# Cosine attention and a leaky-ReLU MLP: weight quarters and four pairs of heads moved in the order of loads

## The chip, the cores and the metric

The kernel runs on one core of one Trainium2 chip. Its metric is the device time of one execution, in microseconds (us), lower is better. Six actors matter: TensorE (PE in the profile, its weight loads PEld), VectorE (DVE), ScalarE (ACT), GpSimd (POOL), SyncE (SP), which only issues transfers, and the 16 DMA engines that carry them out.

## The reference

What is computed, for q, k and v of 8 batches x 12 heads x 448 rows x 64 and an MLP with 768 x 2048 and 2048 x 768 weights:

```python
q_n = q / (np.linalg.norm(q, axis=-1, keepdims=True) + 1e-06)
k_n = k / (np.linalg.norm(k, axis=-1, keepdims=True) + 1e-06)
scores = np.matmul(q_n, k_n.transpose(0, 1, 3, 2)) / tau
attn = np.exp(scores - scores.max(-1, keepdims=True))
attn = attn / (attn.sum(-1, keepdims=True) + 1e-09)
x = np.matmul(attn, v)           # then (batch*row, head*dim) = 3584 x 768
h = x @ w_in
out = np.maximum(0.01 * h, h) @ w_out
```

## The kernel before

**Slots.** A slot is one pair of heads of one batch: 8 batches x 6 pairs are 48 slots, counted from 0, so "the 13th to 16th pair" are slots 12 to 15. Per slot the kernel

- loads q and k: `load_qk(s)` (L119) issues four transfers on SP's queue, the first 384 rows of q, those of k, and the 64 rows that remain of each;
- squares them on POOL: `squares(s)` (L156), which must wait until the slot's loads have landed;
- sums the squares on DVE: `sums(s)` (L169), in two parts, q and k;
- takes the roots on ACT: `roots(s)` (L180), and normalises to bf16 on DVE: `normalise(s)` (L190);
- transposes the result: `transposes(s)` (L226), on TensorE up to slot 9 and by a DMA transpose on SP's queue from slot 10 on;
- multiplies for the scores, three key tiles of 128 rows per slot and one that two slots share, and takes their exponentials on ACT: `key_tiles` (L245).

`hold(x)` (L485) is a one-column copy on POOL that reads a normalised slot. POOL executes in order, so what is written behind it starts no earlier than that slot was normalised.

**Groups.** Two slots make a group of four heads. `load_v(j)` (L138) and `load_v_rem` (L145) load a group's values, cast to bf16 on the way, on POOL's queue. `totals(j)`, `products(j, e)` and `scale(j, e)` make the sums of the exponentials, the products with v and the quotient, which is the MLP's input, transposed.

**Weights.** `load_w_in(i)` (L104) loads a quarter of w_in (768 KB as bf16): quarters 0 and 1 hold the even and the odd row blocks of the first half of its columns, 2 and 3 those of the second half. `load_w_out(half)` (L110) loads half the columns of w_out (1536 KB). Both run on POOL's queue.

**Order of the work.** The order on every engine is written out by hand.

1. A loop over slots s = 0 to 5 (L528 to L588) does the first batch's attention. Iteration s normalises slot s + 1, issues the loads of slot s + 5, squares slot s + 3, and sums slot s + 2; the q part of that sum stands on DVE ahead of the normalisation (L541 to L543). v's groups 1 and 2, w_in's quarters 1 to 3 and both halves of w_out are issued in it too, behind that iteration's squares on POOL (L550 to L557). Group 0 of v and quarter 0 of w_in are issued just ahead of the loop (L513, L514).
2. `firsts(b, begun, between)` (L634) multiplies one "chunk" of x (384 or 512 of the rows of two batches, in turn) by w_in: 16 blocks m of its columns, each with 6 products and one activation on ACT. `between` says what else is put ahead of which m. For batch 0 slots 6 to 9 are normalised in it.
3. `visit(b, order, norms, between)` (L644) multiplies a chunk by w_out in groups of two output blocks of 128 rows and half the columns (`two_groups`, L413). A group goes over the 16 row blocks of w_out twice, and the scores of the next batch's six slots are put between its steps; the scores of slots 12 and 13, and of 14 and 15, against their shared keys come first in visit 1 (L649). After the 4th step of the first `norms` groups, `norm` (L623) normalises one slot, issues the loads of the slot four further on and squares the slot two further on; after the 20th step the next slot is summed (L658 to L661).
4. `attend_batch(b + 1)`, the v loads of the batch after, and `firsts(b + 1, ...)` follow, with further slots normalised (L700 to L715). Then 3 and 4 again.

In visit 0 the first group of two uses w_out's first half only, the second group both halves (L693).

**Buffers.** q and k have four buffers, so slot s + 4 can be loaded once slot s has been normalised; the normalised slots have three, the transposed ones five.

Of the kernel before, what the change touches and what calls it, by code (L numbers as in the profile page):

```python
# [16 lines left out]
def kernel(  # L17
# [23 lines left out]
    MT = D_ff // 128  # L41
    HALF = D_model // 2
# [24 lines left out]
    gp = nc.gpsimd  # L67
# [32 lines left out]
    w_out_sb = cpool.tile([128, MT, D_model], BF16, name="w_out_sb")  # L100
    w_in_r = moe_w_in.rearrange("(j p e) n -> e p j n", p=128, e=2)
    w_out_r = moe_w_out.rearrange("(mo mi) n -> mi mo n", mi=128)

    def load_w_in(i):  # L104
        n0, e = i // 2 * (D_ff // 2), i % 2
        gp.dma_start(
            out=w_in_sb[:, e::2, n0 : n0 + D_ff // 2], in_=w_in_r[e, :, :, n0 : n0 + D_ff // 2]
        )

    def load_w_out(half):  # L110
        n0 = half * HALF
        gp.dma_start(out=w_out_sb[:, :, n0 : n0 + HALF], in_=w_out_r[:, :, n0 : n0 + HALF])

    def main(x, b, h0, nh):
        return x[b, h0 : h0 + nh, 0:MAIN].rearrange("h (p t) d -> p h t d", t=3)
# [3 lines left out]
    def load_qk(s, engs=(nc.sync, nc.sync), rem_eng=None):  # L119
        if s >= NSLOT:  # L120
            return
        b, h0 = s // NPAIR, 2 * (s % NPAIR)
        q_h = ldp.tile([128, 2, 4, D], F32, name="q_h")
        k_h = ldp.tile([128, 2, 3, D], F32, name="k_h")
        engs[0].dma_start(out=q_h[:, :, 0:3], in_=main(q, b, h0, 2))
        engs[1].dma_start(out=k_h, in_=main(k, b, h0, 2))
        for i, (x, eng) in enumerate(zip((q, k), engs)):
            (rem_eng or eng).dma_start(  # L128
                out=q_h[64 * i : 64 * i + 64, :, 3],
                in_=x[b, h0 : h0 + 2, MAIN:S].rearrange("h p d -> p h d"),  # L130
            )
        raw[s] = (q_h, k_h)
# [5 lines left out]
    def load_v(j):  # L138
        if j >= B * NQ:
            return  # L140
        b, jj = divmod(j, NQ)
        vb[j] = vbp.tile([128, 4, 3, D], BF16, name="v_b")
        gp.dma_start(out=vb[j], in_=main(v, b, 4 * jj, 4))  # L143
# [12 lines left out]
    def squares(s, engs=(gp, gp)):  # L156
        if s >= NSLOT:
            return
        tiles = []
        for x, eng, name in zip(raw[s], engs, ("sq0", "sq1")):  # L160
            sq = sqp.tile(list(x.shape), F32, name=name)
            if eng is nc.scalar:
                nc.scalar.activation(sq, x, func=AF.Square)
            else:
                eng.tensor_tensor(sq, x, x, op=ALU.mult)  # L165
            tiles.append(sq)
        sqs[s] = tiles

    def sums(s, parts=(0, 1)):  # L169
        if s >= NSLOT:  # L170
            return
        if s not in ss:
            ss[s] = smp.tile([128, 14], F32, name="ss")
        for i in parts:
            o = ss[s][:, 0:8] if i == 0 else ss[s][:, 8:14]
            nc.vector.tensor_reduce(  # L176
                o.rearrange("p (h t) -> p h t", h=2), sqs[s][i], axis=AX.X, op=ALU.add
            )

    def roots(s):  # L180
        if s >= NSLOT:
            return
        nc.scalar.activation(ss[s], ss[s], func=AF.Ln, bias=tiny)  # L183
        nc.scalar.activation(ss[s], ss[s], func=AF.Exp, scale=0.5)  # L184
        if s < 2:
            nc.scalar.activation(ss[s], ss[s], func=AF.Identity, bias=eps)  # L186
# [55 lines left out]
    def scores(s, kis):  # L242
        key_tiles([(s, ki) for ki in kis])
# [231 lines left out]
    def fill(count):  # L475
        wm = banks(1)
        for i in range(count):
            nc.tensor.matmul(
                out=wm, lhsT=warm[:, :128], rhs=warm, start=(i == 0), stop=(i == count - 1)
            )  # L480
# [4 lines left out]
    def hold(x):  # L485
        seen = smp.tile([128, 1], F32, name="seen")
        gp.tensor_copy(out=seen, in_=x)  # L487
# [21 lines left out]
    normalise(0)  # L509
    load_qk(4)  # L510
    hold(qn[0][:, 6, 0, 0:1])
    squares(2)
    load_v(0)  # L513
    load_w_in(0)  # L514
    dst = qtp.tile([128, 7, 128], BF16, name="qkT")
    qkT[0] = dst.rearrange("p t c -> p (t c)")
# [11 lines left out]
    for s in range(NPAIR):  # L528
        j = s // 2 - 1 if s >= 2 else None
        even = s % 2 == 0  # L530
        n = s + 2 if s + 2 < NPAIR else None
        if s != 3 and s != 5:
            scores(s, (0,))
        if s == 1:
            roots(2)
        if j is not None and not even:
            products(j, 1)
        scores(s, (1,))
        fill(2)
        if s and n:  # L540
            sums(n, (0,))  # L541
        if s < 5:
            normalise(s + 1)  # L543
            load_qk(s + 5)
        if j is not None and not even:
            scale(j, 0)
        if s < 5:
            hold(qn[s + 1][:, 6, 0, 0:1])
            squares(s + 3)
        if s in (1, 2):  # L550
            load_v(s)
        if s == 0:
            load_v_rem(0, slice(2, 4))
        if s < 3:
            load_w_in(s + 1)
        if s in (3, 4):
            load_w_out(s - 3)  # L557
        if n:
            sums(n, (1,))
        scores(s, (2,))  # L560
        if s == 5:

            scale(j, 1)
            for m in range(SOON):
                pms[0, m] = banks(1, (0, m, 0), 4 + m)
            first(0, 0, range(KT - 2))
        elif not even:
            fill(2)
        if not even:
            scores(s, (3,))  # L570
        if s < 5:
            transposes(s + 1)
        if s == 0:
            sums(2, (0,))
        if s == 5:
            first(0, 1, range(KT - 2))
            sums(6)
            sums(7)
        elif not even:
            fill(2)  # L580
        if n and s:
            roots(n)
        if j is not None and not even and s < 5:
            scale(j, 1)
        if j is not None and even:
            totals(j)
            scores(s + 1, (0,))
            products(j, 0)  # L588
# [34 lines left out]
    def norm(s, transposed=True):  # L623
        if s >= NSLOT:
            return
        roots(s)
        normalise(s)
        if transposed:
            transposes(s)
        load_qk(s + 4)  # L630
        hold(qn[s][:, 6, 0, 0:1])
        squares(s + 2)

# [10 lines left out]
    def visit(b, order, norms, between):  # L644


        s0 = (b + 1) * NPAIR
        tiles = [(s0 + p, ki) for p in range(NPAIR) for ki in range(3)]
        key_tiles([(s0 + 1, 3), (s0 + 3, 3)])  # L649
        for i, two in enumerate(order):  # L650
            after = between[i == len(order) - 1]
            for n, _ in enumerate(two_groups(b, two), 1):
                for _ in range(after.get(n, 0)):
                    key_tiles([tiles.pop(0)])
                if not tiles and s0 + 5 not in ended:
                    ended.add(s0 + 5)
                    key_tiles([(s0 + 5, 3)])
                if n == 4 and i < norms:  # L658
                    norm(s0 + 4 + i)
                if n == 20 and i < norms:  # L660
                    sums(s0 + 5 + i)  # L661
        assert not tiles

# [19 lines left out]
    ready = 10  # L683
    for b in range(B):
        tokens = chunk_cols(b)[1] // 128
        if b == B - 1:
            for ts in range(tokens):
                for half in range(2):
                    second(b, ts, half)
            break  # L690
        order = [((ts, 0), (ts, 1)) for ts in range(tokens)]
        if b == 0:
            order = [((0, 0), (1, 0)), ((2, 0), (0, 1)), ((1, 1), (2, 1))]  # L693
        visit(b, order, tokens - 1, three if tokens == 3 else four)
        ready += tokens - 1
        attend_batch(b + 1)
        for j in range((b + 2) * NQ, (b + 3) * NQ):
            load_v(j)
        load_v_rem(b + 2)
        s = ready  # L700
        between = {0: [lambda s=s: norm(s)], 1: [lambda s=s: sums(s + 1)]}
        if tokens == 3:
            between.update({
                4: [lambda s=s: norm(s + 1), lambda s=s: sums(s + 2)],
                7: [lambda s=s: norm(s + 2), lambda s=s: sums(s + 3)],
                10: [lambda s=s: norm(s + 3)], 13: [lambda s=s: sums(s + 4)],
            })
            ready += 4
        else:
            between.update({  # L710
                4: [lambda s=s: norm(s + 1)], 5: [lambda s=s: sums(s + 2)],
                8: [lambda s=s: norm(s + 2)], 12: [lambda s=s: sums(s + 3)],
            })
            ready += 3
        firsts(b + 1, 0, between)  # L715
# [35 lines left out]
```

## Time and profile before

| | us |
|---|---|
| median of 3 runs | 419.67 |
| the three runs | 417.07, 419.67, 420.43 |
| the profiled execution | 417.26 |
| its span, first to last instruction | 415.4 |
| TensorE busy in it | 401.8 (97%) |
| ScalarE busy | 260.1 (63%) |
| VectorE busy | 193.4 (47%) |
| GpSimd busy | 138.1 (33%) |

The trace is of the profiled execution; its instants are counted from the first instruction. TensorE's granted clock is 0.996 of full speed on the mean. A row of the timeline gives start, length, engine, line, operation, what it writes from what it reads, and in brackets how long the engine stood idle before it and what ended that. A row with "SPq", or one on POOL with DMA_DIRECT2D, is the issue of a transfer; the rows "... KB, n" give the time from that issue to the landing. In the chain of waits a DMA's length counts from its issue to its landing.

### The profile page before, as it was taken

What the parts mean: (1) busy time and instruction counts of PE and PEld (TensorE: products, weight loads), DVE (VectorE), ACT (ScalarE), POOL (GpSimd) and SP (SyncE); (2) the same over time, 40 slices, a digit from 0 to 9 for tenths busy, and PEclk for the clock granted to TensorE, in tenths of its full rate; (3) what the DMA queues carried; (4) which work ended last, traced back from release to release, by engine and by line L of the source; (5) the groups of instructions that cost most, each with busy time, mean ns of one, the idle gap of its engine ahead of it and who ended that gap; (6) DMA issues with size and microseconds to landing.
All of it is one profiled execution on the core that took longest, in us unless ns stands there. A gap on an engine that the chain in (4) does not pass through costs nothing.

```text
span 415.4 us, 10159 instructions
## 1 busy us (share of the span) xinstructions
PE 401.8 (97%) x4088; PEld 215.0 (52%) x4099; DVE 193.4 (47%) x412; ACT 260.1 (63%) x448; POOL 138.1 (33%) x209
## 2 busy tenths in 40 slices
PE   8689997999999999999999999999999999999996
PEld 3224655544555555544555555544555565544564
DVE  6865965256352735157261645156362654040021
ACT  4877477745785569845775559855776559934300
POOL 2935457055140634054231533153232530000000
PEclk9999999999999999999999999999999999999999
DMA  6999999886376965576376975576477753210023
GB/s 149 201 220 220 221 221 197 206 114 148 86 191 131 113 156 128 124 116 141 91 177 144 115 172 95 136 110 136 109 171 163 102 97 50 75 39 2 0 76 77
DMA packets 104911, 54.21 MB, mean 130 GB/s; under 512 B 70816, under 2 KB 99872, under 8 KB 104864
## 3 DMA queue, kind: packets, MB, share of 16 engines
q1 hardware_dynamic: 78960, 41.24, 42.8%
q0 software_dynamic: 25056, 11.80, 22.5%
q8 instruction: 32, 0.52, 0.5%
q10 hardware_dynamic: 848, 0.52, 0.4%
q14 instruction: 15, 0.12, 0.1%
HBM read 45.61 MB, written 11.01 MB: 136 GB/s over the span
## 4 chain that ended last, share of the span: by engine, by line
PE 83%; DMA 13%; SPq 1%; DVE 1%; ACT 1%; POOL 0%; issue 0%; POOLq 0%; ACTq 0%
PE ps L355 31%; PE ps L434 29%; PE ps L297 10%; PE ps L257 7%; DMA w_out_sb<-in_moe_w_out_dram 7%; PE ps L392 5%; DMA q_h<-in_k_dram 4%; DMA k_h<-in_k_dram 2%; PE ps L284 1%; SPq L128 1%; POOL sq L165 0%; DVE qn L200 0%; DVE ss L176 0%; ACT ss L183 0%; ACT ss L186 0%
## 5 line engine op out<-in xcount | busy, mean ns | idle before, releaser
L355 PE MATMUL ps<-xT,w_in_sb 128*128 128x384 bf16 (+1 forms) x760 | 147.3, 352 | 0.4
L434 PE MATMUL ps<-w_out_sb,hT 64*128 64x384 bf16 x1536 | 143.5, 323 | 2.1 <-DMA w_out_sb<-in_moe_w_out_dram 2.1
L269 ACT ACTIVATE pe<-ps 128x896 bf16<-128x896 f32 x144 | 123.3, 918 | 22.5 <-PE ps L257 20.8
L362 ACT ACTIVATE hT<-ps 128x384 bf16<-128x384 f32 (+1 forms) x128 | 67.7, 544 | 73.5 <-PE ps L355 73.2
L355 PEld LDWEIGHTS <-w_in_sb 128*128 128x128 bf16 x768 | 74.2, 98 | 71.2 <-issue 3.4
L434 PEld LDWEIGHTS <-hT 64*128 64x128 bf16 x1536 | 75.1, 94 | 56.3 <-issue 5.8
L444 DVE COPY osb<-ps 128x384 f32<-128x384 f32 x48 | 24.5, 553 | 76.9 <-PE ps L434 43.7
L257 PE MATMUL ps<-qkT 64*128 64x448 bf16 (+1 forms) x384 | 55.5, 354 | 3.4 <-ACT pe L269 2.0
L176 DVE TENSOR_REDUCE ss<-sq 128x6 f32<-128x384 f32 (+1 forms) x95 | 54.7, 611 | 4.7 <-POOL sq L165 4.4
L165 POOL TENSOR_TENSOR sq<-q_h 128x512 f32<-128x512 f32 x46 | 48.5, 1055 | 18.1 <-DMA q_h<-in_k_dram 17.4
L487 POOL CAST seen<-qn 128x1 f32<-128x1 bf16 x48 | 8.9, 185 | 124.2 <-DVE qn L200 120.4
L143 POOL DMA_DIRECT2D v_b<-in_v_dram x24 | 18.6, 775 | 66.9 <-PE ps L297 66.9
L195 DVE TENSOR_SCALAR ss<-ss 128x14 f32<-128x14 f32 x46 | 8.2, 178 | 68.5 <-ACT ss L184 68.5
L165 POOL TENSOR_TENSOR sq<-k_h 128x384 f32<-128x384 f32 x46 | 39.0, 848 | 0.0
L332 DVE TENSOR_TENSOR xT<-ps,rb 128x448 bf16<-128x448 f32 x48 | 27.8, 620 | 23.1 <-ACT rb L311 23.0
L200 DVE TENSOR_TENSOR qn<-q_h,r 128x512 bf16<-128x512 f32 x48 | 34.7, 723 | 1.6
L297 PE MATMUL ps<-pe,v_b 128*32 128x448 bf16 x576 | 31.9, 353 | 0.0
L257 PEld LDWEIGHTS <-qkT 64*128 64x128 bf16 (+1 forms) x384 | 17.7, 96 | 23.8 <-issue 11.1
L200 DVE TENSOR_TENSOR qn<-k_h,r 128x384 bf16<-128x384 f32 x48 | 28.8, 600 | 0.0
L310 ACT ACTIVATE rb<-ps 128x448 f32<-128x448 f32 x24 | 12.9, 539 | 24.3 <-PE ps L297 24.3
L398 DVE COPY osb<-ps 128x384 f32<-128x384 f32 (+1 forms) x9 | 4.6, 513 | 36.6 <-issue 22.6
L269 ACT ACTIVATE pr<-ps 128x896 bf16<-128x896 f32 x24 | 21.3, 921 | 0.2 <-PE ps L257 0.2
(49 smaller groups left out, 216.8 us busy)
## 6 DMA issues: line engine op xcount, KB each, us to landing
q_h<-in_q_dram SPq DMA_DIRECT2D x48, 192.0 KB, 3.2
k_h<-in_k_dram SPq DMA_DIRECT2D x46, 192.0 KB, 3.1
out_dram<-osb SPq DMA_DIRECT2D x30, 192.0 KB, 3.0
v_b<-in_v_dram POOLq DMA_DIRECT2D x24, 192.0 KB, 4.7
out_dram<-osb SPq DMA_DIRECT2D x12, 384.0 KB, 2.8
w_in_sb<-in_moe_w_in_dram POOLq DMA_DIRECT2D x4, 768.0 KB, 12.9
w_out_sb<-in_moe_w_out_dram POOLq DMA_DIRECT2D x2, 1536.0 KB, 24.1
q_h<-in_q_dram SPq DMA_DIRECT2D x48, 32.0 KB, 3.8
```

The source lines that it names most:

```text
L165: eng.tensor_tensor(sq, x, x, op=ALU.mult)
L176: nc.vector.tensor_reduce(o.rearrange("p (h t) -> p h t", h=2), sqs[s][i], axis=AX.X, op=ALU.add)
L200: nc.vector.tensor_tensor(qn[s][:, lo:hi], x.rearrange("p h t d -> p t h d"), r[:, r0 : r0 + 2 * nt].rearrange("p (h t) -> p t h", h=2) .u ...
L257: nc.tensor.matmul(out=out[:, a, :S], lhsT=x[rows, c0:c1], rhs=x[rows, 0:S], start=True, stop=True,)
L269: nc.scalar.activation(out=dst, in_=sc[:, :, :S], func=AF.Exp, scale=inv_tau)
L297: nc.tensor.matmul(out=x[32 * g : 32 * g + 32, :S], lhsT=weights(g, ki) if ki < 3 else rem(g), rhs=pe[s][:, ki, a, :] if ki < 3 else pr[j] ...
L332: nc.vector.tensor_tensor(xT[m][:, 2 * jj + e, half * S : (half + 1) * S], pos.pop((j, e))[:, :S], rbs[j], op=ALU.mult,)
L355: nc.tensor.matmul(out=pm[:, :n], lhsT=w_in_sb[:, kt, m * 128 : (m + 1) * 128], rhs=xT[c // 2][:, kt, c0 : c0 + n], start=(kt == 0), stop= ...
L362: nc.scalar.activation(out=hT[c][:, m, :n], in_=pms.pop((c, m))[:, :n], func=AF.Prelu, alpha=0.01)
L392: nc.tensor.matmul(out=po2[:, :n], lhsT=hT[c][:, m, ts * 128 : (ts + 1) * 128], rhs=w_out_sb[:, m, lo : lo + n], start=(m == 0), stop=(m = ...
L434: last[i] = nc.tensor.matmul(out=po2[:, i, :HALF], lhsT=hT[c][rows, m, ts * 128 : (ts + 1) * 128], rhs=w_out_sb[rows, m, half * HALF : (ha ...
L444: nc.vector.tensor_copy(out=osb[c, ts][:, half * HALF : (half + 1) * HALF], in_=po2[:, i, :HALF])
```

## The change

- `load_w_out` can split its half into several transfers, each with a run of the 16 row blocks; the second half is issued in four.
- Group 0 of v is issued ahead of `squares(2)` instead of behind it.
- Quarters 1, 2 and 3 of w_in are issued in iterations 1, 2 and 3 instead of 0, 1 and 2. Group 2 of v is issued in iteration 3 instead of 2. The halves of w_out stay in iterations 3 and 4.
- `norm(8)` and `norm(9)`, in the first `firsts`, no longer issue the loads of slots 12 and 13; `norm(10)` and `norm(11)`, in visit 0, do, where those of slots 14 and 15 were. Slots 14 and 15 load ahead of m = 0 of the second `firsts`.
- The sum of slot 12 leaves visit 0 for m = 1 of that `firsts`, and slots 12 to 15 are normalised ahead of m = 2, 5, 8 and 11, where it was 0, 4, 7 and 10. From slot 16 on all is issued by the same rule as before.

```diff
-    def load_w_out(half):
-        n0 = half * HALF
-        gp.dma_start(out=w_out_sb[:, :, n0 : n0 + HALF], in_=w_out_r[:, :, n0 : n0 + HALF])
+    def load_w_out(half, parts=1):
+        n0, n = half * HALF, MT // parts
+        for m in range(0, MT, n):
+            gp.dma_start(
+                out=w_out_sb[:, m : m + n, n0 : n0 + HALF],
+                in_=w_out_r[:, m : m + n, n0 : n0 + HALF],
+            )
...
     hold(qn[0][:, 6, 0, 0:1])
+    load_v(0)
     squares(2)
-    load_v(0)
     load_w_in(0)
...
-        if s in (1, 2):
-            load_v(s)
+        if s in (1, 3):
+            load_v(s // 2 + 1)
         if s == 0:
             load_v_rem(0, slice(2, 4))
-        if s < 3:
-            load_w_in(s + 1)
-        if s in (3, 4):
-            load_w_out(s - 3)
+        elif s < 4:
+            load_w_in(s)
+        if s == 3:
+            load_w_out(0)
+        elif s == 4:
+            load_w_out(1, 4)
...
-        load_qk(s + 4)
+        if not 8 <= s < 12:
+            load_qk(s + 4)
+        elif s >= 10:
+            load_qk(s + 2)
         hold(qn[s][:, 6, 0, 0:1])
         squares(s + 2)
...
-                if n == 20 and i < norms:
+                if n == 20 and i < norms - (b == 0):
                     sums(s0 + 5 + i)
...
-        if tokens == 3:
+        if b == 0:
+            between = {
+                0: [lambda: load_qk(14), lambda: load_qk(15)],
+                1: [lambda: sums(12)], 2: [lambda: norm(12)],
+                3: [lambda: sums(13)], 5: [lambda: norm(13)],
+                6: [lambda: sums(14)], 8: [lambda: norm(14)],
+                9: [lambda: sums(15)], 11: [lambda: norm(15)], 13: [lambda: sums(16)],
+            }
+            ready += 4
+        elif tokens == 3:
```

## The prediction

> **What bounds the kernel now.** I read the chain that ended last, then the busy time of each engine stage by stage, then the instants at which TensorE waits.
>
> ```profile
> PE 83%; DMA 13%; SPq 1%; DVE 1%; ACT 1%; POOL 0%; issue 0%; POOLq 0%; ACTq 0%
> ```
> ```profile
> 26.38:29.80 3.42, 1.98 (x14) 0.78 (x15) 3.36 (x8) 1.37 (x4) 1.35 (x3) 1.00 1.26 219
> 29.80:33.21 3.41, 3.41 (x27) 1.27 (x25) 1.96 (x4) 2.29 (x3) 2.43 (x3) 0.50 1.12 225
> 33.21:63.80 30.59, 30.41 (x304) 17.05 (x302) 21.30 (x41) 21.34 (x42) 16.26 (x22) 1.00 1.24 221
> 63.80:65.93 2.13, 0.00 (x1) 0.00 (x1) 2.06 (x5) 0.72 (x3) 2.13 (x5) 1.00 1.37 233
> 65.93:106.50 40.57, 40.47 (x397) 21.32 (x402) 19.06 (x38) 24.76 (x42) 16.38 (x24) 1.00 0.88 162
> 106.50:411.90 305.40, 304.99 (x3211) 166.71 (x3216) 128.44 (x277) 190.72 (x323) 83.99 (x127) 1.00 0.54 111
> ```
> ```profile
> 38.46 27.42 DMA w_out_sb<-in_moe_w_out_dram
> 65.93 0.97 PE ps L434 x9
> ```
>
> The columns of a stage are its length, then the busy time of PE, PEld, DVE, ACT and POOL, the granted clock, the DMA share and GB/s. From 65.93 us to the end TensorE is busy 40.47 of 40.57 and 304.99 of 305.40 us: a change can win nothing there, only lose. All that can be won lies before 65.93 us: 2.13 us in which TensorE does nothing until w_out's second half, 27.42 us on its way, has landed; and a head in which it is busy 1.98 of 3.42 us and then works 3.41 us at half clock. DMA moves 219 to 233 GB/s through all of this: the head is a queue for the DMA engines.
>
> **How the two queues share them.** Packets of POOL's queue (q0) and of SP's (q1), from 22 to 26 us beside w_in, and from 40 to 64 us beside w_out:
>
> ```profile
> q0 software_dynamic: 342, 0.66, 87.3%
> q1 hardware_dynamic: 351, 0.20, 22.9%
> ```
> ```profile
> q0 software_dynamic: 4010, 3.07, 81.3%
> q1 hardware_dynamic: 4021, 2.19, 43.0%
> ```
>
> They go one for one. A pair of packets takes 4000/342 = 11.7 ns beside w_in and 24000/4010 = 6.0 ns beside w_out. A slot (one pair of heads) is 2 x 192 KB in rows of 768 B and 2 x 32 KB in rows of 256 B, 768 packets. So a q/k load is slow when w_in lies beside it, which is what the order of issues decides.
>
> **Part 1: w_out's second half.** Slots 12 and 13 no longer load in front of it: 1536 packets. SP's part of a pair is 43.0/(81.3 + 43.0) = 35% of 6.0 ns, 2.1 ns, so 3.2 us of traffic leave, and the half would land near 62.7 us even whole. In quarters, the first four of its sixteen row blocks land some three quarters of its 12.4 us of service (its landing at 65.9 less that of the first half, below) earlier. TensorE asks at 63.80. The wait of 2.1 us goes: **-2.1**, with both causes covering it. If the head below wins time, TensorE asks earlier; the quarters cover that.
>
> w_out's first half must be there at 57.12, where its products begin:
>
> ```profile
> 32.81 1.21 POOL L112 DMA_DIRECT2D w_out_sb<-in_moe_w_out_dram  x1
> ...
> 38.46 1.20 POOL L112 DMA_DIRECT2D w_out_sb<-in_moe_w_out_dram  x1
> 43.28 0.18 POOL L487 CAST seen<-qn 128x1 f32<-128x1 bf16 x1 [3.62 <-DVE ss L195]
> ```
> ```profile
> w_out_sb<-in_moe_w_out_dram POOLq DMA_DIRECT2D x1, 1536.0 KB, 20.7
> ```
>
> ```profile
> 57.12 0.99 PE L434 MATMUL ps<-w_out_sb,hT 64*128 64x384 bf16 x10
> ```
>
> It lands at 32.81 + 20.7 = 53.5, 3.6 us early. The bytes ahead of it in its queue stay the same, so I leave it there. Three more issues on POOL cost between nothing and 3 x 1.20 = 3.6 us; behind them stand slot 6's hold and slot 8's squares, and POOL idles 3.62 us just there: 0.
>
> The price of a transfer, whatever its size, could speak against quarters. Four small loads issued back to back at 84.48 us:
>
> ```profile
> 84.48 2.45 POOL L150 DMA_DIRECT2D v_rem<-in_v_dram  x4
> ```
> ```profile
> v_rem<-in_v_dram POOLq DMA_DIRECT2D x2, 32.0 KB, 3.4
> ```
>
> All four are issued within 2.45 us and each lands some 3.4 us after its own issue, so they overlap; I take 0 for the split, and 3 x 3.4 = 10.2 us as the far end. The Trainium skill ("DMA: Bandwidth & Descriptors", Anatomy of one DMA) puts a fixed 2.0 us on every DMA; three more in a row would make 6.0 us by it, the last quarter near 68.7. The trace's overlapping landings do not bear out adding them up.
>
> **Part 2: the head.** Slot 0's v load (L513) now issues before squares(2), so w_in(0), at 12.35 us today, issues some 0.7 us sooner: v's issue (0.8 us) is out from between. Then it stands ahead of slot 4's last transfer, and w_in(1), which ran beside slot 5's, stands an iteration later. What these two loads do today:
>
> ```profile
> 12.15 0.60 SPq L128 DMA_DIRECT2D q_h<-in_k_dram  x1
> ...
> 14.61 0.66 SPq L128 DMA_DIRECT2D q_h<-in_k_dram  x1
> ```
> ```profile
> q_h<-in_k_dram SPq DMA_DIRECT2D x1, 32.0 KB, 3.7
> ```
> ```profile
> q_h<-in_k_dram SPq DMA_DIRECT2D x1, 32.0 KB, 9.5
> ```
> ```profile
> 12.35 0.76 POOL L106 DMA_DIRECT2D w_in_sb<-in_moe_w_in_dram  x1
> ...
> 17.51 1.03 POOL L165 TENSOR_TENSOR sq<-q_h 128x512 f32<-128x512 f32 x1
> ...
> 24.24 1.03 POOL L165 TENSOR_TENSOR sq<-q_h 128x512 f32<-128x512 f32 x1 [3.09 <-DMA q_h<-in_k_dram]
> ```
> ```profile
> 20.42 0.81 PE L214 MATMUL ps<-id,qn 128*128 128x128 bf16 x7 [0.39 <-DVE qn L200]
> ...
> 27.16 0.81 PE L214 MATMUL ps<-id,qn 128*128 128x128 bf16 x7 [1.15 <-DVE qn L200]
> ```
> ```profile
> 18.58 0.69 DVE L176 TENSOR_REDUCE ss<-sq 128x8 f32<-128x512 f32 x1 [0.34 <-POOL sq L165]
> ...
> 25.31 0.69 DVE L176 TENSOR_REDUCE ss<-sq 128x8 f32<-128x512 f32 x1 [3.41 <-POOL sq L165]
> ```
> ```profile
> 26.06 0.92 ACT L269 ACTIVATE pr<-ps 128x896 bf16<-128x896 f32 x1
> 28.60 0.31 ACT L183 ACTIVATE ss<-ss,tiny 128x14 f32<-128x14 f32 x1 [1.62 <-DVE ss L176]
> ```
>
> Slot 4 lands at 12.15 + 3.7 = 15.9, slot 5 at 14.61 + 9.5 = 24.1. DVE sums slot n+1 before it normalises slot n, so a late load stops the slot before it: 3.41 us at 25.31 for slot 5. ACT, which runs without a pause up to 26.98, then waits 1.62 us.
>
> After the change slot 4 lands between 15.9 (as now) and 12.15 + 9.5 = 21.7 (treated as slot 5 is). I take 18.5: q/k issue ahead of w_in(0) and go first, the remainders (256 packets) go beside it at 11.7 ns, 3.0 us. Its squares then start at 18.65 instead of 17.51, and everything up to ACT's 26.98 moves by 1.1, to 28.1: the new stall is at slot 3's transposition, 0.39 + 1.1 us. Slot 5 follows slot 4 with no w_in beside it; with the 3.7 us that slot 4 takes so, it lands near 22.2, not 24.1, and slot 4's transposition is ready 27.16 - 24.24 = 2.9 us after its squares start, at 25.3, before TensorE comes to it. The wait of 1.62 us goes, and ACT goes on at 28.1 instead of 28.60: **-0.5**. The ends: slot 4 as now gives 26.98 for 28.60, -1.6; slot 4 at 21.7 moves the start to 21.85, 4.3 late, and ACT to 31.3, +2.7.
>
> The half-clock stretch costs between 0 and half of its 3.41 us, 1.7; I put it at 1.2, since TensorE is busy throughout. I leave it where it is, for the head has a stall of the same kind in either kernel. The Trainium skill ("TensorE: Matmul & The Clock Gate", Part 1) has the clock halved after an idle window of about 3.4 us. Here it was halved after a window in which TensorE was busy 1.98 of 3.42 us, so this trace is stricter; by the Trainium skill's rule the new stall of 1.5 us could not halve it.
>
> Part 3: the other values. Today's v(2):
>
> ```profile
> 26.02 0.80 POOL L143 DMA_DIRECT2D v_b<-in_v_dram  x1
> ```
> ```profile
> v_b<-in_v_dram POOLq DMA_DIRECT2D x1, 192.0 KB, 10.7
> ```
> ```profile
> 39.02 0.74 PE L297 MATMUL ps<-pe,v_b 128*32 128x448 bf16 x12
> ```
>
> It lands at 36.7 and is used at 39.02. It now issues behind squares(6). Its queue holds the same bytes ahead of it, so if that queue stays fed it lands between 36.7 and, with 32.81 (after squares(6) today) for its issue, 43.5. Slot 6 no longer has w_in(1) ahead, so I put its issue near 29 and its landing near 38: 0.
>
> **Part 4: slots 12 to 15.** They load and are normalised beside TensorE's work; only the end is tight. Slot 15 is normalised at m = 11, not 10, of 16, and transposed by DMA for the scores at 106.46.
>
> ```profile
> 85.63 20.89 PE L355 MATMUL ps<-xT,w_in_sb 128*128 128x512 bf16 x94
> 106.46 0.57 PE L257 MATMUL ps<-qkT 64*64 64x448 bf16 x8
> ```
> ```profile
> 101.98 1.26 SPq L232 DMA_TRANSPOSE qkT<-qn  x1
> ```
> ```profile
> qkT<-qn SPq DMA_TRANSPOSE x1, 2.9
> ```
>
> It lands at 104.9, 1.6 us early; one m is 20.89/16 = 1.3 us. 0.3 us remain: I take **+0.1**, at most 1.3. Squares(12) and (13) now make POOL wait for their loads in the visit; behind them are only the v loads for the next batch but one.
>
> **The sum.** -2.1 - 0.5 + 0.1 = -2.5 us. The profiled execution took 417.26 us, 2.4 less than the median of 419.67: 414.8 on its own time, **417.2** against the median.
>
> **The rivals.**
> - Slot 4 is not delayed: -2.1 - 1.6 + 0.1 = -3.6, 416.1, and with the half-clock stretch gone, -4.8, 414.9. For it: slot 4's first three transfers issue before w_in(0). Against: packets go one for one as soon as w_in runs. 0.25.
> - Slower: slot 4 is treated as slot 5 is today, lands at 21.7, and slot 3's transposition waits 4.3 + 0.39 us, long enough for a second half-clock stretch: -2.1 + 2.7 + 1.2 + 0.1 = +1.9, 421.6. It decides from a landing of about 20, where delay and stretch together eat 2.0 us. For it: 9.5 us against 3.7. 0.13.
> - A new wait for v(2): issued at 29 and again 10.7 us on its way, it lands at 39.7, 1.2 after TensorE asks (38.5): -1.3, 418.4. 0.10.
> - The quarters add up: 62.7 + 10.2 = 72.9. The last one is needed after 24 of that group's products, at 63.8 - 0.5 + 24 x 0.97/9 = 65.9: 7.0 late, +4.5, 424.2. The overlapping landings speak against it. 0.02.
>
> The forecast has 0.50. The change could fail to do what it says only if a quarter could not be used alone; products with w_out begin at 57.12 while its second half lands at 65.9, so parts are used as they land, and Part 1 doesn't need the split.
>
> **The numbers.** Within 1% (4.2 us, about what a measurement of this kernel tells from no change) are the forecast, v(2) and most of the first two rivals. Over 1% faster is below 415.5: about half of the first rival and a tail of the forecast, 0.20. Over 1% slower, above 423.9: quarters and a tail of the slower rival, 0.04. The range 414.5 to 421.0 takes in all but the ends of the rivals.
>
> **What would show it.** The wait for w_out gone from TensorE's list; slot 4's last transfer 6 us on its way instead of 3.7, slot 5's about 7.5 instead of 9.5; slot 3's transposition waiting about 1.5 us, slot 4's none; no wait for v or at 104 us. It is wrong if the half-clock stretches change in number, or if TensorE waits for v(2).

## The result, and the profile after

| us | before | after |
|---|---|---|
| median of 20 runs each, in turn | 419.00 | 416.38 |
| lowest and highest | 416.90, 420.44 | 415.13, 417.68 |
| the profiled execution | 417.26 | 416.94 |

The ratio is 0.9947 [0.9931, 0.9963]: 2.2 us (1.6 to 2.9) of 419, half a per cent. The two profiled executions differ by 0.3 us only: that of before was one of its shortest, that of after one of its longer ones. So the pair of traces shows where the time goes, but not the size of the gain.

From the page of after: its span, the chain that ended last, and the group of the products with w_out.

```profile
span 415.2 us, 10161 instructions
...
PE 92%; DMA 3%; DVE 2%; ACT 1%; issue 0%; POOL 0%; SPq 0%; POOLq 0%
...
L438 PE MATMUL ps<-w_out_sb,hT 64*128 64x384 bf16 x1536 | 142.8, 323 | 0.0
```

DMA holds 3% of the chain instead of 13%, and the products with w_out (L438, L434 before) have no idle time ahead of them at all. The stages of after, with the columns of before: length; PE, PEld, DVE, ACT and POOL busy; granted clock; DMA share; GB/s.

```profile
18.30:21.71 3.41, 1.46 (x8) 0.41 (x8) 1.42 (x5) 2.74 (x4) 2.34 (x3) 1.00 1.18 268
21.71:28.54 6.83, 6.26 (x59) 2.33 (x59) 5.33 (x11) 2.45 (x5) 5.78 (x10) 0.50 1.02 180
28.54:64.22 35.68, 34.78 (x341) 18.65 (x342) 23.88 (x47) 25.85 (x49) 19.60 (x27) 1.00 1.20 207
64.22:105.58 41.36, 41.26 (x408) 20.56 (x406) 20.49 (x42) 26.76 (x46) 18.15 (x28) 1.00 0.92 170
105.58:411.00 305.42, 304.71 (x3207) 166.44 (x3213) 128.44 (x276) 190.90 (x323) 84.00 (x127) 1.00 0.54 112
```

The stage without TensorE at 63.80 us is gone. The head is worse: 6.83 us at half clock where before had 3.41. TensorE's rows that matter, first what it waits for and where the work with each weight begins:

```profile
22.28 0.97 PE L218 MATMUL ps<-id,qn 128*128 128x128 bf16 x7 [1.97 <-DVE qn L204]
...
37.99 0.82 PE L359 MATMUL ps<-xT,w_in_sb 128*128 128x384 bf16 x4
...
58.69 0.99 PE L438 MATMUL ps<-w_out_sb,hT 64*128 64x384 bf16 x10
...
84.75 2.12 PE L359 MATMUL ps<-xT,w_in_sb 128*128 128x512 bf16 x8
...
105.58 0.38 PE L261 MATMUL ps<-qkT 64*64 64x448 bf16 x4
106.36 0.38 PE L261 MATMUL ps<-qkT 64*64 64x448 bf16 x4 [0.40 <-DMA qkT<-qn]
```

The same instants of both traces make the ledger of the pair:

| TensorE begins | before | after | after is |
|---|---|---|---|
| products with w_in of batch 0 | 36.44 | 37.99 | 1.55 late |
| products with w_out | 57.12 | 58.69 | 1.57 late |
| second `firsts` | 85.63 | 84.75 | 0.88 early |
| scores in visit 1 | 106.46 | 105.58 | 0.88 early |
| the last of these scores | no wait | 106.36 | waits 0.40 |

The wait of 2.13 us before w_out's second half is gone, but 1.57 us were lost ahead of it; with some 0.3 us won elsewhere, 0.88 is left.

The transfers, first those that answer to the 3.7 and 9.5 us of slots 4 and 5, then w_out's quarters: the row of their four issues, and the time from issue to landing of the first quarter and of the last.

```profile
q_h<-in_k_dram SPq DMA_DIRECT2D x1, 32.0 KB, 7.2
```
```profile
q_h<-in_k_dram SPq DMA_DIRECT2D x1, 32.0 KB, 8.0
```
```profile
37.75 3.05 POOL L113 DMA_DIRECT2D w_out_sb<-in_moe_w_out_dram  x4
```
```profile
w_out_sb<-in_moe_w_out_dram POOLq DMA_DIRECT2D x1, 384.0 KB, 19.6
```
```profile
w_out_sb<-in_moe_w_out_dram POOLq DMA_DIRECT2D x1, 384.0 KB, 23.4
```

Slot 4's last transfer, issued at 12.02, lands at 19.2; slot 5's, issued at 14.57, at 22.6. The first quarter of w_out's second half lands at 37.75 + 19.6 = 57.3, and the last, issued at 40.03, at 63.4: the second group, which begins near 65, has it all.

### The profile page after: what moved, and what is told of

The parts are those of the page before. It is cut to its first block, busy times and chain, and to the rows that moved or that the text cites. A ratio compares the mean times of both kernels' runs of the same rounds, so it can differ in the third digit from the quotient of the medians.

```text
span 415.2 us, 10161 instructions
## 1 busy us (share of the span) xinstructions
PE 402.2 (97%) x4088; PEld 213.8 (51%) x4099; DVE 192.2 (46%) x412; ACT 260.5 (63%) x448; POOL 139.0 (33%) x212
## 4 chain that ended last, share of the span: by engine, by line
PE 92%; DMA 3%; DVE 2%; ACT 1%; issue 0%; POOL 0%; SPq 0%; POOLq 0%
PE ps L359 35%; PE ps L438 30%; PE ps L301 12%; PE ps L261 8%; PE ps L396 5%; DMA q_h<-in_k_dram 2%; PE ps L288 1%; DMA k_h<-in_k_dram 1%; PE ps L218 1%; DMA qkT<-qn 1%; ACT pe L273 1%; DVE qn L204 0%; DVE ss L180 0%; POOL sq L169 0%; ACT pr L273 0%
## 5 line engine op out<-in xcount | busy, mean ns | idle before, releaser
L438 PE MATMUL ps<-w_out_sb,hT 64*128 64x384 bf16 x1536 | 142.8, 323 | 0.0
L273 ACT ACTIVATE pe<-ps 128x896 bf16<-128x896 f32 x144 | 123.5, 918 | 22.2 <-PE ps L261 20.2
L438 PEld LDWEIGHTS <-hT 64*128 64x128 bf16 x1536 | 73.6, 94 | 54.8 <-issue 3.2
L261 PE MATMUL ps<-qkT 64*128 64x448 bf16 (+1 forms) x384 | 54.3, 355 | 4.0 <-ACT pe L273 2.3
L199 DVE TENSOR_SCALAR ss<-ss 128x14 f32<-128x14 f32 x46 | 9.2, 201 | 65.8 <-ACT ss L188 65.8
L147 POOL DMA_DIRECT2D v_b<-in_v_dram x24 | 18.5, 775 | 59.8 <-PE ps L301 59.8
L204 DVE TENSOR_TENSOR qn<-q_h,r 128x512 bf16<-128x512 f32 x48 | 33.3, 693 | 1.6
L301 PE MATMUL ps<-pe,v_b 128*32 128x448 bf16 x576 | 33.1, 362 | 0.0
L261 PEld LDWEIGHTS <-qkT 64*128 64x128 bf16 (+1 forms) x384 | 16.8, 96 | 24.9 <-issue 11.2
L301 PEld LDWEIGHTS <-v_b 128*32 128x32 bf16 x576 | 15.4, 99 | 12.6 <-issue 1.4
L402 DVE COPY osb<-ps 128x384 f32<-128x384 f32 (+1 forms) x9 | 4.6, 513 | 36.6 <-issue 22.6
```

Of the source, the lines that this page charges most:

```text
L204: nc.vector.tensor_tensor(qn[s][:, lo:hi], x.rearrange("p h t d -> p t h d"), r[:, r0 : r0 + 2 * nt].rearrange("p (h t) -> p t h", h=2) .u ...
L261: nc.tensor.matmul(out=out[:, a, :S], lhsT=x[rows, c0:c1], rhs=x[rows, 0:S], start=True, stop=True,)
L273: nc.scalar.activation(out=dst, in_=sc[:, :, :S], func=AF.Exp, scale=inv_tau)
L301: nc.tensor.matmul(out=x[32 * g : 32 * g + 32, :S], lhsT=weights(g, ki) if ki < 3 else rem(g), rhs=pe[s][:, ki, a, :] if ki < 3 else pr[j] ...
L438: last[i] = nc.tensor.matmul(out=po2[:, i, :HALF], lhsT=hT[c][rows, m, ts * 128 : (ts + 1) * 128], rhs=w_out_sb[rows, m, half * HALF : (ha ...
```

## The experiments

Each kernel was timed in turn with the kernel before, whose median was 418.62, 418.50 and 417.54 us in the three sets; kernels of different sets are compared by their ratios. The theory at the start was that of the prediction: Part 1 makes the gain, the head gives a little, Part 4 nothing. The rivals were that the split alone does it, that the head costs time, and that the half-clock windows are what it costs.

### One part alone on the kernel before

**Quarters alone (e2_split_only).** `load_w_out(s - 3)` becomes

```diff
-            load_w_out(s - 3)
+            load_w_out(s - 3, 1 if s == 3 else 4)
```

> The kernel before with w_out's second half in four transfers and nothing else. Theory (quarters are used as they land, a transfer's own latency overlaps): first quarter near 57, last near 66, the wait of 2.1 us before the second group of visit 0 falls to under 0.5; 1.6 to 2.1 us faster, ratio 0.995 to 0.996. Rival (each transfer pays its latency in turn): last quarter past 70, a wait of several us, ratio above 1.005.

416.86 us, ratio 0.9973 [0.9947, 0.9998]: 1.1 us faster (0.1 to 2.2), where 1.6 to 2.1 were expected. In its profile the quarters land at 56.2, 59.4, 62.4 and 65.4, and TensorE does not wait for them. But in that execution it began with w_out 2.58 us later than before:

```profile
59.70 0.99 PE L438 MATMUL ps<-w_out_sb,hT 64*128 64x384 bf16 x10
```

It came to the second half only near 66.3, when even the whole half, at 65.9 before, would have been there. So this trace does not show that the split removes the wait. The one that shows a quarter used before the rest has landed is e13's (below): TensorE came to the second half near 61.8, its last quarter landed at 63.3, and there was no wait for it.

**Slots 12 to 15 alone (e3_pairs_only).** The edits of `norm`, of `norms - (b == 0)` and of `between` for batch 0, as in the diff of the change; w_out's half whole, the head as before.

> The kernel before with only slots 12 to 15 loaded, summed and normalised later. Theory (3.2 us of traffic leave the front of w_out's second half): it lands near 62.7 in one piece, the wait of 2.1 us goes, and 0.4 us come back as the wait for slot 15's transposition in visit 1: 1.5 to 2 us faster, ratio 0.995 to 0.9965. Rival (the engines give the freed time to other loads): w_out lands within 1 us of 65.9, ratio 0.998 to 1.001.

415.86 us, ratio 0.9941 [0.9918, 0.9964]. TensorE's waits for w_out and in visit 1:

```profile
63.62 0.97 PE L434 MATMUL ps<-w_out_sb,hT 64*128 64x384 bf16 x9 [1.04 <-DMA w_out_sb<-in_moe_w_out_dram]
...
105.64 0.38 PE L257 MATMUL ps<-qkT 64*64 64x448 bf16 x4 [1.11 <-DMA qkT<-qn]
```

The whole half lands at 63.6 instead of 65.9, though the first half, ahead of it in the queue, landed 0.8 us later than before (54.3): from one landing to the other it took 9.3 us instead of 12.4. So 3.1 us of traffic left its way, close to the 3.2 estimated. Another 1.11 us is lost where slot 15's transposition is now late.

**Both (e11_pairs_split).** The two edits above together: after, with the head of before.

> The kernel before with slots 12 to 15 later and w_out's second half in quarters, the head's order as before. Theory (the later w_in quarters win about 1 us in the head, worth something only now that w_out no longer waits; group 0 of v costs about 1.5 to 2 in the changed kernel): between the changed kernel (0.9947) and the one with group 0 of v back (0.9912): ratio 0.992 to 0.9945. Rival (the later quarters win nothing): 0.9905 to 0.9915.

415.62 us, ratio 0.9933 [0.9907, 0.9960]. No wait for w_out in its profile, which is of its slowest execution. Between this and the changed kernel lies only the head, and that one's 0.9947 is 0.6 us more, though the intervals overlap.

**The whole head alone (e4_head_only).** v's group 0 ahead of `squares(2)`, w_in and v(2) an iteration later, nothing else.

> The kernel before with only the new order of v and w_in in the head, w_out in two whole halves, slots 12 to 15 as before. Theory (w_out's landing sets when the second group of visit 0 starts, so the head's loss or gain is swallowed by that wait): start of the second group within 1 us of 65.9, ratio 0.998 to 1.002. Rival (the change's gain sits in the head, which in the kernel before is often worse than in the profiled execution): ratio 0.994 to 0.996.

421.28 us, ratio 1.0073 [1.0048, 1.0097]: slower than before, which neither the theory nor the rival had. TensorE's two long waits:

```profile
23.10 0.97 PE L218 MATMUL ps<-id,qn 128*128 128x128 bf16 x7 [3.08 <-DVE qn L204]
...
68.61 0.97 PE L438 MATMUL ps<-w_out_sb,hT 64*128 64x384 bf16 x9 [2.32 <-DMA w_out_sb<-in_moe_w_out_dram]
```

Slot 4's last transfer took 8.0 us, slot 3's transposition waited 3.08 us, and w_out's second half landed at 68.6 instead of 65.9. The wait for it did not shrink although TensorE itself was late: the weights were later still. POOL's issue of w_in's quarter 1, before and in the changed kernel (22.78 in e4):

```profile
16.29 0.77 POOL L106 DMA_DIRECT2D w_in_sb<-in_moe_w_in_dram  x1
```
```profile
21.95 0.75 POOL L106 DMA_DIRECT2D w_in_sb<-in_moe_w_in_dram  x1
```

Quarter 0 landed at 20.7 in after. Before, quarter 1 stood behind it in the queue; in after nothing did but a v load issued at 21.14. POOL's queue ran dry: from 21.0 to 21.9 us it moved 71 packets, where before it moved 235. What it did not carry then it carries later, ahead of w_out.

**The later w_in without the sooner v (e9_win_only).** As e4, but with `load_v(0)` behind `squares(2)`.

> The kernel before with w_in's quarters 1 to 3 and group 2 of v one iteration later, and nothing else. Theory (the slot that reads late, slot 5, no longer has w_in(1) beside it; group 0 of v is what cost the head): slot 4 near 16 to 18, slot 5 near 22.5, no or one half-clock stretch, and the wait for w_out grows by what the head wins, since w_out lands no sooner than 65.9: ratio 0.997 to 1.002. Rival (the later quarters starve POOL's queue and cost by themselves, as in the head-only version): w_out's second half lands past 67.5, ratio 1.004 to 1.008.

419.39 us, ratio 1.0028 [1.0009, 1.0047]. The wait for w_out, and the window in which it ends:

```profile
66.18 1.75 PE L438 MATMUL ps<-w_out_sb,hT 64*128 64x384 bf16 x9 [3.67 <-DMA w_out_sb<-in_moe_w_out_dram]
```
```profile
65.12:68.53 3.41, 2.35 (x16) 1.33 (x17) 1.76 (x4) 0.19 (x1) 2.46 (x4) 0.50 1.49 143
```

In this execution the head was quick: slot 4 landed as before, TensorE reached w_out at 55.84 instead of 57.12, and asked for the second half at 62.5. That the later w_in won this isn't shown, for e3's profile, with the head of before, reached w_out at 55.91. The half landed at 66.1, 0.3 us later than before, so the 1.3 us came back as a longer wait, and with the wait came 6.8 us at half clock, up to 71.95. A gain in the head is worth something only once Part 1 is in. Here quarter 1 was issued at 20.67, before quarter 0 had landed (20.9): the queue stayed fed, and e4's 68.6 did not come about.

### One part taken back from after

**The v load back (e1_v0_back).**

```diff
-    load_v(0)
     squares(2)
+    load_v(0)
     load_w_in(0)
```

> The changed kernel with group 0 of v issued behind squares(2) again, all else as changed. Theory (early v(0) brings w_in(0) ahead of slot 4's remainders and so costs the head): slot 4's last transfer lands near 16 instead of 19.2, slot 3's transposition waits about 0.4 us instead of 1.97, at most one half-clock stretch; 1.5 to 2.5 us faster than the changed kernel, ratio to the kernel before 0.989 to 0.991. Rival (slot 4 is late because w_in(0) itself is in front, wherever v(0) stands, and only the later w_in quarters matter): slot 4 stays near 19, ratio as the changed kernel's, 0.9947.

414.86 us (six runs, 414.06 to 415.87), ratio 0.9912 [0.9879, 0.9945]. Slot 4's last transfer took 4.1 us, slot 3's transposition waited 0.40 us, and there was no window at half clock. Three new waits stood in its profile, these two and 0.70 us at 54.22 for a slot's normalisation:

```profile
37.73 0.75 PE L301 MATMUL ps<-pe,v_b 128*32 128x448 bf16 x12 [0.87 <-DMA v_b<-in_v_dram]
...
105.29 0.38 PE L261 MATMUL ps<-qkT 64*64 64x448 bf16 x4 [1.07 <-DMA qkT<-qn]
```

So the sooner v costs about 1.5 us in the changed kernel (0.9947 against 0.9912; the intervals overlap a little), and 1.9 without the other parts (1.0073 against 1.0028). TensorE now waits for v(2): the rival "a new wait for v(2)" is real as soon as the head is quick (0.87 us in e9 too).

**The half in one transfer (e5_unsplit).**

```diff
-            load_w_out(1, 4)
+            load_w_out(1)
```

> The changed kernel with w_out's second half in one transfer again. Theory (the traffic that left is enough): it lands near 63.4, where the last quarter landed, TensorE asks near 65; no wait, same as the changed kernel, ratio to the kernel before 0.993 to 0.997. Rival (the quarters carry the gain): a wait of over 1 us comes back, ratio 0.998 or more.

416.69 us, ratio 0.9963 [0.9945, 0.9981], which can't be told from the changed kernel. The half landed at 64.2 and TensorE did not wait. Once the traffic has left, the quarters add nothing that shows.

### The suspected costs by themselves

**Half clock (e10_fill).** Six filler products ahead of slot 3's transposition keep TensorE busy through the stall.

```diff
+        if s == 2:
+            fill(6)
         if s < 5:
             transposes(s + 1)
```

> The changed kernel with six filler products (512 columns of ones, 1.3 us at full clock) put ahead of slot 3's transposition, where TensorE waits 1.97 us. Theory (the half-clock stretch follows from a window in which TensorE was busy under about 60%, and costs about 1.2 us each): the window before it is busier, no stretch or one instead of two, 1.2 to 2.4 us faster than the changed kernel, ratio 0.989 to 0.992. Rival (the clock does not follow this wait, or the work behind it is ScalarE's): same number of stretches or same time, ratio 0.994 to 0.996.

417.07 us, ratio 0.9963 [0.9941, 0.9986]: not faster than the changed kernel, against the theory. The stretch from 18 to 36 us, first in after and then in e10 (the granted clock is the third figure from the end), then what TensorE waited for:

```profile
18.00:36.00 18.00, 14.72 (x138) 5.36 (x141) 10.32 (x22) 11.93 (x20) 10.97 (x16) 0.81 1.10 212
```
```profile
18.00:36.00 18.00, 15.90 (x168) 6.15 (x167) 12.19 (x26) 14.01 (x23) 10.98 (x15) 1.00 1.08 204
```
```profile
39.62 0.75 PE L301 MATMUL ps<-pe,v_b 128*32 128x448 bf16 x12 [1.42 <-DMA v_b<-in_v_dram]
...
56.41 0.34 PE L218 MATMUL ps<-id,qn 128*128 128x128 bf16 x3 [0.70 <-DVE qn L204]
...
107.26 0.38 PE L261 MATMUL ps<-qkT 64*64 64x448 bf16 x4 [0.86 <-DMA qkT<-qn]
```

Both half-clock windows are gone, TensorE begins with w_in at 35.43 instead of 37.99, and nothing is left of it at w_out: 59.13 against 58.69. The time went into waits for v(2), for a slot's normalisation and for slot 15. In this kernel, then, half clock in the head cost nothing that shows: without it TensorE comes sooner to waits that the loads and normalisations set.

**Slot 15 sooner (e6_m10).** Slots 12 to 15 normalised ahead of m = 1, 4, 7, 10 instead of 2, 5, 8, 11.

> The changed kernel with slots 12 to 15 normalised one m sooner (1, 4, 7, 10). Theory (slot 15's transposition lands 1.3 us sooner, and TensorE waits 0.4 us for it at 106 us): that wait goes, 0.3 to 0.5 us faster than the changed kernel, ratio 0.9935 to 0.994. Rival (ScalarE and VectorE are the limit there, the earlier step only waits longer): the transposition lands within 0.3 us of 106.3, ratio unchanged.

417.07 us, ratio 0.9977 [0.9963, 0.9992]: no gain. DVE's last normalisation of slot 15, and SP's queue around its transposition, first in after and then in e6:

```profile
101.61 0.55 DVE L204 TENSOR_TENSOR qn<-k_h,r 128x384 bf16<-128x384 f32 x1
```
```profile
99.40 1.26 SPq L236 DMA_TRANSPOSE qkT<-qn  x1
100.76 0.53 SPq L129 DMA_DIRECT2D q_h<-in_q_dram  x1
101.38 0.43 SPq L130 DMA_DIRECT2D k_h<-in_k_dram  x1
101.86 0.63 SPq L132 DMA_DIRECT2D q_h<-in_q_dram  x1
102.54 0.60 SPq L132 DMA_DIRECT2D q_h<-in_k_dram  x1
103.25 1.26 SPq L236 DMA_TRANSPOSE qkT<-qn  x1
```
```profile
100.95 0.55 DVE L204 TENSOR_TENSOR qn<-k_h,r 128x384 bf16<-128x384 f32 x1
```
```profile
102.62 0.60 SPq L132 DMA_DIRECT2D q_h<-in_k_dram  x1
103.33 1.26 SPq L236 DMA_TRANSPOSE qkT<-qn  x1
```

DVE was done 0.7 us sooner and the transposition issued no sooner, because SP was not free. A slot is five issues on SP's queue, 1.26 + 0.53 + 0.43 + 0.63 + 0.60 = 3.45 us and 3.85 us from one transposition to the next: from 91.25 us, where slot 12's transposition is issued, SP issues without a pause, and slot 15's transposition stands behind three such rows. It is so in e1, e5, e11 and e12 too: SP is free 0.1 us before it issues slot 15's, and slot 15 is normalised over 1 us before that.

**Another order on SP's queue (e12_sp_order).** It was meant to put slot 18's loads behind slot 15's transposition.

```diff
+        if s == 15:
+            load_qk(18)
-        if not 8 <= s < 12:
+        if s != 14 and not 8 <= s < 12:
             load_qk(s + 4)
         elif s >= 10:
             load_qk(s + 2)
```

> The changed kernel with the loads of slot 18 issued behind slot 15's transposition instead of ahead of it. Theory (SyncE, not the m at which slot 15 is normalised, set that transposition: its queue issues without a pause from 91 us on): it issues near 102.2 instead of 103.25 and lands near 105.2, TensorE's wait of 0.4 us goes; 0.3 to 0.5 us faster than the changed kernel, ratio 0.9935 to 0.9945. Rival (ScalarE and VectorE set it): it lands within 0.3 us of 106.3.

417.20 us, ratio 0.9972 [0.9951, 0.9992]. It did not do what it was meant to: for s = 14 the `elif` holds, so slot 16 was loaded a second time there. The page counts the loads, 49 of them where after has 48:

```profile
q_h<-in_q_dram SPq DMA_DIRECT2D x49, 192.0 KB, 3.2
```

Four issues stood ahead of the transposition as before, and it went out at 103.27. The run says nothing on the order of the queue.

### The best of the parts

**e7_best.** After, with v's group 0 back behind `squares(2)`, v(2) back in iteration 2, and slot 12 begun at m = 0:

```diff
-        if s in (1, 3):
-            load_v(s // 2 + 1)
+        if s in (1, 2):
+            load_v(s)
...
-                0: [lambda: load_qk(14), lambda: load_qk(15)],
-                1: [lambda: sums(12)], 2: [lambda: norm(12)],
-                3: [lambda: sums(13)], 5: [lambda: norm(13)],
-                6: [lambda: sums(14)], 8: [lambda: norm(14)],
-                9: [lambda: sums(15)], 11: [lambda: norm(15)], 13: [lambda: sums(16)],
+                0: [lambda: load_qk(14), lambda: load_qk(15), lambda: sums(12), lambda: norm(12)],
+                1: [lambda: sums(13)], 3: [lambda: norm(13)],
+                4: [lambda: sums(14)], 6: [lambda: norm(14)],
+                7: [lambda: sums(15)], 9: [lambda: norm(15)], 13: [lambda: sums(16)],
```

> The changed kernel with group 0 of v behind squares(2) and group 2 in iteration 2 as before, and slots 12 to 15 normalised at m = 0, 3, 6, 9. Theory: against the version with group 0 alone moved back (0.9912), the wait of 0.9 us for v(2) and that of 1.1 us for slot 15's transposition go too: ratio 0.987 to 0.9885. Rival (each wait removed lets the next, w_out's, in its place): ratio 0.990 to 0.991, with a wait on w_out of over 1 us.

412.84 us, ratio 0.9882 [0.9861, 0.9903], the fastest. Its middle stage:

```profile
62.00:104.00 42.00, 42.00 (x420) 20.97 (x416) 20.60 (x43) 27.33 (x48) 18.80 (x29) 1.00 0.93 179
```

TensorE is busy 42.00 of 42.00 us: slot 15's transposition is issued at 99.94 and is there in time, and v(2) lands at 32.4. The three waits that e1 had left are gone, 0.87 + 0.70 + 1.07 = 2.64 us; e7 is 2.0 us faster by the medians and 1.3 by the ratios, whose intervals overlap. How much each of the two edits behind this gave was not measured apart. The head is no better in this profile: slot 4's last transfer took 6.1 us, and slot 3's transposition waited 1.50.

**w_in's quarter 0 later still (e13_best_win0_late).** e7 with `load_w_in(0)` behind `squares(3)`.

> The fastest version so far (0.9882) with w_in's quarter 0 moved behind squares(3) too. Theory (slot 4 loads in 3.7 us when no w_in is beside it): slot 4 lands by 16.3, slot 3's transposition no longer waits 1.5 us, 0.3 to 1 us faster than that version, ratio 0.986 to 0.9875. Rival (POOL's queue runs dry by as much as the quarter is late and w_out comes later by it): w_out's last quarter past 64 with a wait on it, ratio 0.988 to 0.991.

414.40 us, ratio 0.9911 [0.9886, 0.9936]: no better than e7, and likely worse. Slot 5's last transfer, with w_in's quarter 0 issued 1.3 us behind it, and TensorE's waits:

```profile
q_h<-in_k_dram SPq DMA_DIRECT2D x1, 32.0 KB, 3.0
```
```profile
55.24 0.99 PE L438 MATMUL ps<-w_out_sb,hT 64*128 64x384 bf16 x10 [0.80 <-DMA w_out_sb<-in_moe_w_out_dram]
...
72.36 0.55 PE L261 MATMUL ps<-qkT 64*128 64x448 bf16 x4 [1.11 <-DMA qkT<-qn]
```

The head is quicker, 3.0 us for slot 5 instead of 9.5, and the weights are later: w_out's first half now lands behind its need.

## Why the prediction was right, and where it was not

The time was forecast at 417.2 us and is 416.4; -2.5 us was summed, and the ratio makes it 2.2 (1.6 to 2.9). The sum holds better than its terms, and that is in part luck.

**Part 1 (-2.1): right, and the size fits.** The wait is gone. That the traffic does it is shown: the half lands 2.3 us sooner without slots 12 and 13 ahead of it (e3), and without the split nothing is lost in the changed kernel (e5). With a quicker head the traffic alone leaves 1.04 us (e3), and there the quarters can help (e13). That the split alone covers the wait, as the prediction had it, isn't shown; alone it gave 1.1 us (e2). The quarters do not add up their latencies: the four landed some 2 us apart, 6.1 us from first to last. Parts 1 and 4 together gave 0.9933, 2.8 us (1.7 to 3.9), where -2.0 was forecast (e11).

**Part 2 (-0.5): the landings were near, the step after them was not right.** Slot 4 was put at 18.5 and landed at 19.2, slot 5 at 22.2 and landed at 22.6; slot 3's transposition was to wait 1.5 us and waited 1.97, and slot 4's none. Slot 5's landing was right by luck. It was to follow slot 4 by 3.7 us with no w_in beside it, but w_in's quarter 0 was under way until 20.7; where slot 4 landed at 16.3 and 15.8 (e1, e9), slot 5 still landed at 22.7 and 22.6, and only with quarter 0 issued behind it, at 15.87, did it land at 17.6 (e13). In the profiled pair the step that failed is "I leave it where it is" on the half-clock stretch. ScalarE was to go on at 28.1; its rows in after, behind the new stall:

```profile
28.85 1.75 ACT L273 ACTIVATE pe<-ps 128x896 bf16<-128x896 f32 x2 [1.97 <-PE ps L261]
30.54 0.92 ACT L273 ACTIVATE pr<-ps 128x896 bf16<-128x896 f32 x1
31.36 0.30 ACT L187 ACTIVATE ss<-ss,tiny 128x14 f32<-128x14 f32 x1
```

Slot 5's roots, at 28.60 before, came at 31.36 instead of 28.1. The exponential that ran at 26.06 ran at 30.54, 4.5 us late instead of 1.1, since TensorE worked through the products ahead of those scores at half clock, and ScalarE waited 1.97 us for it. The slower rival had put ScalarE at 31.3 for a landing of 21.7; half clock made it so at 19.2. The prediction named the sign of this failure: the half-clock stretches changed in number. With a landing of 20.0, the point from which that rival was to decide, e4 was slower by 3.1 us. As the price of the head in the medians this is not shown, though. By the mean granted clock (last section) the changed kernel had 1.35 half-clock windows an execution and the kernel before 1.48, so that the pair's one more is a matter of these two executions, and e10, without any, was no faster.

By the Trainium skill ("TensorE: Matmul & The Clock Gate", Part 1), which wants an idle window of about 3.4 us, neither the stall of 1.97 us in after nor that of 3.08 in e4 halves the clock. The runs are stricter: after a window with TensorE busy 1.46 of 3.41 us it was halved.

**A step of Part 1 failed with the head.** "The bytes ahead of it in its queue stay the same, so I leave it there" holds only while the queue is fed. The late `squares(4)` held POOL up, POOL's queue ran dry for want of quarter 1, and w_out's first half landed 0.6 us later in after (54.1), its second half 2.7 later in e4 (68.6). That is most of e4's 3.1. In the changed kernel the margins of Part 1 hide it. In all, the head as changed costs 3.1 us by itself (e4), where -0.5 was forecast, and about 0.6 in the changed kernel (after against e11, intervals overlapping); what makes the 0.6, if it is there, stays open. The rival that left slot 4 undelayed is what e1 built. Its 414.9 without half clock and the 414.86 measured agree by luck: against its own kernel before e1 gave 3.7 us (2.3 to 5.1), where that rival had 4.8, with the v(2) of the third rival as a part of what is missing.

**Part 3 (0): right.** v(2) was put at 29 for its issue and 38 for its landing; it was issued at 28.46, landed at 38.1, and TensorE did not wait for it. With a quicker head it did (e1, e9, e10).

**Part 4 (+0.1, at most 1.3): the bound held, the reason did not.** The prediction moved slot 15 by one m. It is SP's queue that sets it: five issues per slot, and the rows of three slots stand ahead of slot 15's transposition. The wait was 0.40 us in after and 0.54 to 1.26 in the profiles of e1, e3, e5, e6, e10, e11 and e12. Only an earlier start took it away (e7, e13).

**Why the sum still held.** By the medians Parts 1 and 4 were worth a little more than forecast, and the head cost instead of giving; the two errors partly cancel. On the profiled execution's own time the sum was 414.8 and after's took 416.94, 2.1 us off; against the median it was right since the profile of before was a short execution, as the prediction had corrected for, and that of after was not.

## What to carry to other kernels

When a queue's wait is removed, ask first which landing pins the end: a head that brought TensorE to w_out 1.3 us sooner only lengthened the wait there (e9). A transfer that is moved ahead moves the issues behind it on that engine (w_in's came 1 us sooner) and can put a long load in front of a short one, so write down the instants at which the two queues issue, and how far apart they are. And price a head from several executions: one profile of it is one throw.

## What the runs showed of the hardware

**A race of a tenth of a microsecond.** Slot 4's last transfer (SP's queue) and w_in's quarter 0 (POOL's queue) issue within a microsecond of each other in all profiles but e13's. The issues of e3 and of e11, both with the head of before, and the landing in each:

```profile
12.18 0.60 SPq L128 DMA_DIRECT2D q_h<-in_k_dram  x1
12.52 0.76 POOL L106 DMA_DIRECT2D w_in_sb<-in_moe_w_in_dram  x1
```
```profile
q_h<-in_k_dram SPq DMA_DIRECT2D x1, 32.0 KB, 4.0
```
```profile
11.75 0.76 POOL L106 DMA_DIRECT2D w_in_sb<-in_moe_w_in_dram  x1
11.75 0.60 SPq L132 DMA_DIRECT2D q_h<-in_k_dram  x1
```
```profile
q_h<-in_k_dram SPq DMA_DIRECT2D x1, 32.0 KB, 7.4
```

All fourteen profiles fall in line:

| w_in's issue against slot 4's last | profiles | slot 4's last transfer takes |
|---|---|---|
| 0.11 to 0.34 us behind | before, e1, e2, e3, e9 | 3.7 to 4.2 us |
| 0.00 and 0.01 behind | e11, e7 | 7.4 and 6.1 us |
| 0.52 to 0.73 ahead (v sooner) | after, e4, e5, e6, e10, e12 | 7.2 to 8.0 us |
| 3.7 behind | e13 | 4.1 us |

The change moved w_in's issue by about 1 us and fell on the far side every time; the head of before lies so near the edge that it falls on either. That this makes the spread of the kernel before (416.6 to 421.4 us over 85 executions in the experiments) is likely and not shown, since the timed executions carry no trace. A kernel that holds the order without delaying w_in by an iteration, as e13 does, was not tried.

**What half clock goes with.** A window of 3.41 us at half clock takes 3.41 x 0.5 / 415 = 0.0041 off the mean granted clock, so that mean tells about how many windows an execution had. The kernel before took 417.6 us on average with none (7 executions), 418.0 with one (40), 418.5 with two (28) and 420.1 with three (10); after took 416.1 with one (13) and 416.8 with two (7). A window goes with 0.4 to 0.7 us, not the 1.2 that the prediction gave it, except the third. The count does not say where a window lies: in e5, e9 and e12 one lay between 13.5 and 17.2 us. Five times a second window followed although TensorE had been busy 2.35 to 2.84 of 3.41 us in the first (e9, e4, e2, e6 and after).
